# Block-sparse attention and mixture of experts on one core: the second half's dense tile moved to fourth place, and values stored batch by batch

## The chip, the cores and the metric

The kernel runs on one core of a Trainium2 chip. The metric is device time in microseconds (us), the median over runs. The core has a matrix engine (PE, its weight loads are listed as PEld), three engines for element-wise work (DVE, ACT, POOL), a queue engine SP that issues most transfers, and 16 DMA engines that carry them out.

## What is computed

The reference chains two parts. The first is attention over 4 batches, 8 heads, 768 tokens and head size 64, with a mask by blocks of 32 tokens (24 blocks): a block of queries sees its neighbours, the first and the last block, and three blocks that `sampled_blocks` names for it. The first and the last block of queries see everything.

```python
mask = np.abs(blk_i - blk_j) <= window
mask = mask | (blk_i == 0) | (blk_j == 0) | (blk_i == n_blocks - 1) | (blk_j == n_blocks - 1)
for qb in range(n_blocks):
    for kb in sampled_blocks[qb]:
        mask[qb * block:(qb + 1) * block, kb * block:(kb + 1) * block] = True
...
return np.matmul(attn, v).astype(np.float32)
```

The second part takes each of the 3072 output rows (512 wide), picks the best of 8 experts by gate logits plus a bias of the row's modality, and sends the row through that expert's two layers, scaled by the gate's weight.

```python
logits = x @ w_gate + modality_bias[modality_id]
e_idx = np.argmax(logits, axis=1)
...
    h = np.maximum(x[mask] @ w1[e], 0.0)
    out[mask] = gate_w[mask, None] * (h @ w2[e])
```

## The kernel before, in words

**Tiles.** The rows are cut into 24 tiles of 128 rows, 12 for each half, a half being two of the four batches. One tile of a half is dense: the first and the last block of both batches, with scores against all 768 keys. The other 11 are sparse: two neighbouring blocks of queries of both batches, m = 0 to 10. `tau_of` (L1236) numbers the tiles: the dense tile of a half is its tile 0, sparse tile m is tile m + 1.

**Items and stages.** The attention part is one list, `items` (L1249 to L1254), and the prediction uses an item's place t in it as a clock. The 8 dense items of the first half (2 batches with 4 pairs of heads each) stand at t = 0 to 7. Then come the 88 sparse items, four for each sparse tile, and the 8 dense items of the second half are put between them, two at a time, behind the sparse items that `DENSE_AFTER` lists. Before the change they stand at t = 30, 31, 40, 41 (batch 2) and 58, 59, 62, 63 (batch 3). Each item passes through stages at fixed distances, `LAG`: S scores, M the maximum, X the exponential, T transposes, A the copy out of PSUM, W and V the products with the values, O the division, Y and G the gate. In one step t every stage works on the item that is due, in the order `ORDER`. A dense item's product with the values (`dense_weigh`, L446, matmuls L451) comes 7 steps after its scores (L401); its transposes are L433. A sparse tile's scores are L557, its transposes L582, its products with the shared value blocks L604 (5 steps on) and with its own sampled blocks L613 (7 steps on).

**Loads.** SP issues them in program order; a load whose buffer is still in use holds back all that stand behind it. Keys and values of a batch for the dense tile are loaded whole: keys in 6 pieces (`dense_k`, L159), values in 6 pieces of 256 KB in rows of 2048 bytes (`dense_v`, L165). For the second half `DENSE_IN` says at which t the first of each six is issued, two steps apart. The keys of a batch also feed `share_k` (L480), where POOL copies key blocks for the sparse tiles, from t = 54 for the second half. A sparse tile's value blocks go into one of two buffers: `fetch_v` (L505, two blocks at L516 and L517, more for m = 0 and 1 at L511 to L514) and `fetch_own` (L539, six sampled blocks at L545), each block 128 KB. Values lie in memory as token, batch, feature, so that a block's row holds both batches of a half and is 4096 bytes. `fetch_v` for a tile stands 8 steps after the last item of the tile two before it, and waits for that tile's L613, which reads the same buffer.

**Routing.** When both tiles of a pair (2k, 2k + 1) have been gated, `routing` (L640) picks their experts, stores their rows to `x_d` and ranks them. After 16 tiles the fullest expert is chosen and its first 256 rows form an early group, and after 18 tiles a second one (`choose`, L1091), so that expert work starts before attention ends. `rows_of` (L1055) turns the rank table into row numbers to gather and row numbers to store, on DVE, three times (twice for 2 columns, once for 38). Behind the attention part PE multiplies expert groups of 256 rows without a break (L810 to L812, L825 to L827).

Of the kernel before, what the change touches and what calls it, by code (L numbers as in the profile page):

```python
# [15 lines left out]
ALU = mybir.AluOpType  # L16
# [4 lines left out]
P = 128  # L21
B, H, S, D = 4, 8, 768, 64
BLK = 32
NB = S // BLK
NPAIR = H // 2
HD = H * D
# [3 lines left out]
NT = NTOK // P  # L30
# [8 lines left out]
HB = 2  # L39
# [18 lines left out]
DENSE_DVE = ((0, 0), (0, 1))  # L58
DENSE_AFTER = (21, 29, 45, 47)
LAG = {'d': {'S': 0, 'M': 1, 'X': 2, 'T': 4, 'A': 4, 'W': 7, 'O': 8, 'V': 101, 'Y': 11, 'G': 13}, 's': {'S': 0, 'M': 1, 'X': 2, 'T': 4, 'A': 4, 'W': 5, 'V': 7, 'O': 8, 'Y': 10, 'G': 13}}  # L60
# [13 lines left out]

DENSE_IN = ((19, 14, 30), (49, 38, 44))
Q_IN = 22
# [14 lines left out]
def attention_moe(ctx, tc, kD, qD, qH, v0, v1, blocks, modality, w_gate, bias, w1, w2, out):  # L91
    nc = tc.nc
# [29 lines left out]
    with ExitStack() as actx:  # L122
# [13 lines left out]
        kd, vd = {}, {}  # L136
        KD_SLOT, VD_SLOT = (0, 1, 2, 9), (2, 3, 3, 3)
        ad = slot(4)
# [22 lines left out]
        def dense_v(b, ts=(0, 3), n=3):  # L161
            if b not in vd:
                vd[b] = slot(VD_SLOT[b])[:, 0:3072].rearrange("p (t f) -> p t f", t=6)
            for t in ts:
                nc.sync.dma_start(vd[b][:, t:t + n, :], vH[b // HB][t * P:(t + n) * P, b % HB].rearrange("(t p) f -> p t f", p=P))  # L165

# [336 lines left out]


        def fetch_v(m, half):  # L505
            i, g = 2 * m + 1, half * NM + m
            vg = vbuf[g % 2]
            vrow = vH[half].rearrange("(j s) b f -> s j (b f)", s=BLK)
            if m < 2:
                for n, j in ((0, 0), (1, NB - 1)):  # L510
                    nc.sync.dma_start(vg[32 + 32 * n:64 + 32 * n, 1, :], vrow[:, j, :])  # L511
            if m == 0:
                nc.sync.dma_start(vg[0:32, 1:3, :], vrow[:, i:i + 3:2, :])
                nc.sync.dma_start(vg[96:P, 0:2, :], vrow[:, i - 1:i + 2:2, :])  # L514
                return
            nc.sync.dma_start(vg[0:32, 2, :], vrow[:, i + 2, :])  # L516
            nc.sync.dma_start(vg[96:P, 1, :], vrow[:, i + 1, :])  # L517

# [20 lines left out]
        def fetch_own(m, half, n):  # L539
            i, g = 2 * m + 1, half * NM + m  # L540
            vg = vbuf[g % 2]
            vrow = vH[half].rearrange("(j s) b f -> s j (b f)", s=BLK)
            for k in ((0, 2, 1), (2, 0, 1))[n]:
                reg = own[g][3 * n + k]
                nc.sync.dma_start(vg[32 * (k + n):32 * (k + n) + 32, 2 * n, :], vrow[:, bass.ds(reg, 1), :].rearrange("p j f -> p (j f)"))  # L545

# [508 lines left out]
        def rows_of(tp, n, g_, s_, hold=None):  # L1055
            i_, f_ = ((lambda name, dt=dt: small.tile([P, NCOL], dt, name=name, bufs=1)[:, 0:n]) for dt in (I32, F32))
            pad, tf, to = f_("pad"), f_("tf"), f_("to")
            tk, tb, tn = i_("tk"), i_("tb"), i_("tn")
            nc.vector.tensor_scalar(to, tp[:, 0:n], 0.5, float(NTOK // 2 - 1), ALU.is_lt, ALU.add)
            yield  # L1060
            nc.vector.tensor_tensor(g_, tp[:, 0:n], to, ALU.add)
            if hold is not None:
                ready[NEAR] = True
                while not hold:
                    yield
            yield
            nc.vector.tensor_scalar(pad, tp[:, 0:n], 0.0, 8192.0, ALU.is_equal, ALU.mult)
            nc.vector.tensor_scalar(tk, g_, 7, None, ALU.logical_shift_right)
            yield
            nc.vector.tensor_scalar(tn, g_, 5, 1, ALU.logical_shift_right, ALU.bitwise_and)  # L1070
            nc.vector.tensor_scalar(tf, tk, float(NB // 2), float(-NB // 2), ALU.is_ge, ALU.mult)
            yield
            nc.vector.tensor_scalar(tb, g_, 6, 1, ALU.logical_shift_right, ALU.bitwise_and)
            nc.vector.tensor_tensor(tf, tf, tk, ALU.add)
            yield
            nc.vector.scalar_tensor_tensor(pad, tb, float(S - 2 * BLK), pad, ALU.mult, ALU.add)
            nc.vector.tensor_tensor(to, tf, tn, ALU.add)
            yield
            nc.vector.tensor_scalar(to, to, 0.5, float(S), ALU.is_le, ALU.mult)
            yield  # L1080
            nc.vector.scalar_tensor_tensor(to, tf, float(-2 * BLK), to, ALU.mult, ALU.add)
            yield
            nc.vector.scalar_tensor_tensor(to, g_, float(-BLK), to, ALU.add, ALU.add)
            yield
            nc.vector.tensor_tensor(s_, to, pad, ALU.add)
# [150 lines left out]
        def tau_of(m, half):  # L1236
            return half * (NT // 2) + m + 1

        def end_tile(m, half):
            tau = tau_of(m, half)  # L1240
            gate(tau, turns.pop((m, half)))
            gated.add(tau)
            if tau ^ 1 in gated:
                t = tau - tau % 2
                fillers.append(routing(t, lgs.pop(t), [xrs.pop((t % (NT // 2) + n - 1, half)) for n in range(2)]))

# [262 lines left out]
```

## Time and profile before

| | us |
|---|---|
| median of 3 runs | 526.32 |
| lowest and highest of them | 525.06, 530.39 |
| the profiled execution, whole | 523.66 |
| its span, first to last instruction | 521.9 |
| PE busy in the span | 499.5 |

The profile records one execution. Durations in the prediction are its own, and are set against its 523.66 us, of which 1.76 us lie outside the span. "issue" as the reason of an idle time means that the engine waited for nothing that the profile shows.

### The profile page before, as it was taken

To read this page: it belongs to the slowest core of one execution; us is meant where nothing else is said; L and a number is where in the kernel's file an instruction comes from. 1 tells how busy PE (TensorE), PEld (TensorE's weight loads), DVE (VectorE), ACT (ScalarE), POOL (GpSimd) and SP (SyncE) were. 2 spreads that over 40 slices of the span, in tenths; PEclk is the share of its full clock that TensorE was granted. 3 is DMA by queue.
4 is the path that set the end of the run, shared out by engine and by line. 5 is a ranking of instruction groups with operands and counts; after the bars stand their busy time and mean duration, and the time that the engine had idled before them with its cause. 6 is when DMAs were issued, how large, how long until landed. Compare 5 with 4: busy or idle time off the path is not lost.

```text
span 521.9 us, 18958 instructions
## 1 busy us (share of the span) xinstructions
PE 499.5 (96%) x7124; PEld 420.6 (81%) x7124; DVE 388.4 (74%) x1136; ACT 335.5 (64%) x765; POOL 244.9 (47%) x514
## 2 busy tenths in 40 slices
PE   7999999989899999899999999999999999999995
PEld 5667776767778777688989798998989899898974
DVE  5886688686689899967986868667686766768573
ACT  3799787978789978844545655555565545655561
POOL 6779685576458884312275051323324222241423
PEclk9999999999999999999999999999999999999999
DMA  8997885999756778965878797879669696877860
GB/s 293 332 249 227 241 222 184 244 228 258 196 174 191 207 219 245 273 192 200 242 281 294 246 297 258 266 233 301 200 240 284 227 295 202 280 223 251 260 209 25
DMA packets 59063, 123.84 MB, mean 237 GB/s; under 512 B 9681, under 2 KB 17618, under 8 KB 58962
## 3 DMA queue, kind: packets, MB, share of 16 engines
q1 hardware_dynamic: 54704, 108.88, 68.7%
q0 software_dynamic: 4256, 13.65, 7.9%
q8 instruction: 58, 0.95, 0.8%
q14 instruction: 43, 0.35, 0.3%
q10 hardware_dynamic: 2, 0.00, 0.0%
HBM read 105.97 MB, written 12.86 MB: 228 GB/s over the span
## 4 chain that ended last, share of the span: by engine, by line
PE 73%; DMA 11%; DVE 7%; ACT 3%; SPq 2%; issue 2%; POOL 0%; DVEq 0%; POOLq 0%; ACTq 0%
PE bank L810 8%; PE bank L812 8%; PE bank L811 8%; PE bank L827 7%; PE bank L826 7%; PE bank L825 7%; PE bank L557 6%; PE bank L582 6%; DMA slot<-x_d,gi 5%; PE bank L604 3%; PE bank L613 3%; PE bank L451 2%; DMA slot<-w 2%; PE bank L630 2%; PE bank L401 2%
## 5 line engine op out<-in xcount | busy, mean ns | idle before, releaser
L755 DVE TENSOR_TENSOR slot<-slot 128x1024 fp32r<-128x1024 f32 x99 | 124.6, 1272 | 63.1 <-ACT slot L752 54.9
L752 ACT CAST slot<-slot 128x1024 fp32r<-128x1024 f32 x104 | 107.0, 1047 | 68.3 <-PE bank L811 49.5
L810 PE MATMUL bank<-slot 128*128 128x256 f32 x384 | 108.4, 282 | 0.2 <-issue 0.2
L812 PE MATMUL bank<-slot 128*128 128x256 f32 x384 | 107.9, 281 | 0.1
L811 PE MATMUL bank<-slot 128*128 128x256 f32 x384 | 107.6, 280 | 0.0
L573 ACT ACTIVATE a<-y,mn 128x256 f32<-128x256 f32 x176 | 88.7, 511 | 7.9 <-DVE mn L565 7.7
L846 POOL DMA_INDIRECT out<-slot,si x20 | 27.3, 1364 | 109.5 <-ACT slot L842 106.5
L827 PE MATMUL bank<-slot 128*128 128x512 f32 x192 | 75.9, 395 | 0.4 <-DVE slot L818 0.4
L826 PE MATMUL bank<-slot 128*128 128x512 f32 x192 | 75.9, 395 | 0.0
L825 PE MATMUL bank<-slot 128*128 128x512 f32 x192 | 75.8, 395 | 0.0
L810 PEld LDWEIGHTS bank<-slot 128*128 128x128 f32 x384 | 72.3, 188 | 0.6
L811 PEld LDWEIGHTS bank<-slot 128*128 128x128 f32 x384 | 72.2, 188 | 0.6
L812 PEld LDWEIGHTS bank<-slot 128*128 128x128 f32 x384 | 72.2, 188 | 0.3 <-DVE slot L755 0.3
L565 DVE CUSTOM_DVE_ANT_1 y<-bank,smask 128x256 f32<-128x256 f32 x176 | 66.2, 416 | 0.5 <-PE bank L557 0.3
L502 POOL COPY slot<-slot 128x128 f32 x264 | 63.6, 293 | 0.0
L527 POOL TENSOR_SCALAR slot<-slot 32x1024 f32<-32x1024 f32 x40 | 41.7, 1042 | 33.2 <-issue 12.8
L587 ACT COPY at<-bank 128x512 f32<-128x512 f32 x88 | 50.6, 576 | 9.0 <-PE bank L582 9.0
L582 PE MATMUL bank<-ident,a 128*128 128x128 f32 x352 | 52.1, 280 | 3.0 <-issue 2.2
L557 PE MATMUL bank<-slot,q_raw 64*32 64x256 f32 x1408 | 48.7, 382 | 0.0
L582 PEld LDWEIGHTS bank<-ident,a 128*128 128x128 f32 x352 | 38.1, 141 | 7.3 <-issue 2.3
L827 PEld LDWEIGHTS bank<-slot 128*128 128x128 f32 x192 | 36.1, 188 | 9.2 <-DVE slot L818 0.9
L826 PEld LDWEIGHTS bank<-slot 128*128 128x128 f32 x192 | 36.0, 188 | 8.3 <-DVE slot L755 0.4
(307 smaller groups left out, 859.8 us busy)
## 6 DMA issues: line engine op xcount, KB each, us to landing
slot<-w SPq DMA_DIRECT2D x100, 512.0 KB, 5.2
slot<-v SPq DMA_DIRECT2D x180, 128.0 KB, 4.0
x_d<-xr SPq DMA_DIRECT2D x22, 256.5 KB, 4.2
q_raw<-qH SPq DMA_DIRECT2D x22, 256.0 KB, 4.8
slot<-v SPq DMA_DIRECT2D x16, 256.0 KB, 5.1
slot<-slot SPq DMA_DIRECT2D x120, 32.0 KB, 4.4
slot<-kD SPq DMA_DIRECT2D x13, 256.0 KB, 3.6
slot<-v SPq DMA_DIRECT2D x4, 768.0 KB, 12.4
```

What stands on the lines that cost most here:

```text
L557: nc.tensor.matmul(sp[u][32 * pr:32 * pr + 32, b * 256:(b + 1) * 256], lhsT=q[r, b * NPAIR + pr, n, :], rhs=kv[r, s0:s0 + 8, b, pr, :], st ...
L565: nc.vector.tensor_tensor_reduce(y[:, u, :].rearrange("p (s f) -> p s f", s=8), sp[u][:, b * 256:(b + 1) * 256].rearrange("p (s f) -> p s ...
L573: nc.scalar.activation(a[:, u, :], y[:, u, :], AF.Exp, bias=mn[:, u:u + 1], scale=-1.0, accum_out=total[:, u:u + 1])
L582: nc.tensor.transpose(tp[:, k:k + P], a[:, u, c * P:(c + 1) * P], ident)
L752: nc.scalar.copy(h, s)
L755: (eng or (nc.gpsimd if n in POOL_SPLITS else nc.vector)).tensor_tensor(l, s, h.bitcast(F32), ALU.subtract)
L810: nc.tensor.matmul(o, lhsT=h[:, fs], rhs=xh[g % 2][:, c, :], start=c == 0 and f % 2 == 0, stop=False)
L811: nc.tensor.matmul(o, lhsT=h[:, fs], rhs=xl[g % 2][:, c, :], start=False, stop=False)
L812: nc.tensor.matmul(o, lhsT=l[:, fs], rhs=xh[g % 2][:, c, :], start=False, stop=c == 3 and f % 2 == 1)
L825: nc.tensor.matmul(o, lhsT=hh[0][:, f, ts_], rhs=h[:, fs], start=f == 0, stop=False)
L826: nc.tensor.matmul(o, lhsT=hh[0][:, f, ts_], rhs=l[:, fs], start=False, stop=False)
L827: nc.tensor.matmul(o, lhsT=hl[f // 4][:, f % 4, ts_], rhs=h[:, fs], start=False, stop=f == 7)
```

## The change

Three things are edited together. The dense tile of the second half becomes tile 3 of its half (tau 15 instead of 12), and its items stand at t = 44, 45, 52, 53 (batch 2) and 64, 65, 68, 69 (batch 3); its loads have other times, and the values of batch 3 go to another buffer (slot 0, that of batch 0's keys, instead of slot 3, that of batch 2's values). Values lie in memory as batch, token, feature, so each block's row is two rows of 2048 bytes for all loads of `fetch_v` and `fetch_own`, and the two loads of two blocks each for m = 0 become four of one block. `rows_of` has to undo the other numbering of tiles, with seven more DVE instructions in each call.

```diff
-DENSE_AFTER = (21, 29, 45, 47)
+DENSE_AFTER = (35, 41, 51, 53)
+DENSE_PLACE = (0, 3)
-DENSE_IN = ((19, 14, 30), (49, 38, 44))
+DENSE_IN = ((38, 14, 20), (57, 26, 32))
-        KD_SLOT, VD_SLOT = (0, 1, 2, 9), (2, 3, 3, 3)
+        KD_SLOT, VD_SLOT = (0, 1, 2, 9), (2, 3, 3, 0)
...
-                nc.sync.dma_start(vd[b][:, t:t + n, :], vH[b // HB][t * P:(t + n) * P, b % HB].rearrange("(t p) f -> p t f", p=P))
+                nc.sync.dma_start(vd[b][:, t:t + n, :], vH[b // HB][b % HB, t * P:(t + n) * P].rearrange("(t p) f -> p t f", p=P))
...
+        def vblock(half, j):
+            rows = vH[half].rearrange("b (j s) f -> s b j f", s=BLK)
+            return rows[:, :, bass.ds(j, 1) if not isinstance(j, int) else slice(j, j + 1), :].rearrange("s b j f -> s b (j f)")
...
+            def rows_in(r, c, j):
+                nc.sync.dma_start(vg[r, c, :].rearrange("p (b f) -> p b f", b=HB), vblock(half, j))
...
-                nc.sync.dma_start(vg[32 * (k + n):32 * (k + n) + 32, 2 * n, :], vrow[:, bass.ds(reg, 1), :].rearrange("p j f -> p (j f)"))
+                nc.sync.dma_start(vg[32 * (k + n):32 * (k + n) + 32, 2 * n, :].rearrange("p (b f) -> p b f", b=HB), vblock(half, reg))
...
+            d, first = DENSE_PLACE[1], NT // 2
+            nc.vector.tensor_scalar(dj, tk, float(first), None, ALU.is_ge)
+            yield
+            nc.vector.tensor_scalar(to, tk, float(first + d), float(-d - 1), ALU.is_ge, ALU.mult)
+            nc.vector.tensor_tensor(dj, dj, to, ALU.add)
+            nc.vector.tensor_scalar(to, tk, float(first + d + 1), float(d), ALU.is_ge, ALU.mult)
+            nc.vector.tensor_tensor(dj, dj, to, ALU.add)
             nc.vector.scalar_tensor_tensor(pad, tb, float(S - 2 * BLK), pad, ALU.mult, ALU.add)
             nc.vector.tensor_tensor(to, tf, tn, ALU.add)
+            nc.vector.tensor_tensor(to, to, dj, ALU.add)
...
+            nc.vector.scalar_tensor_tensor(to, dj, float(2 * BLK), to, ALU.mult, ALU.add)
...
-            return half * (NT // 2) + m + 1
+            return half * (NT // 2) + (DENSE_PLACE[half] if m < 0 else m + (m >= DENSE_PLACE[half]))
```

How the order of instructions moves is shown at three places. The first is on PE, around the products with its own value blocks of the first half's last sparse tile (t = 62). Before, the row L613 is that product, L401 are dense scores, L433 dense transposes, L557 and L582 scores and transposes of sparse items:

```order
L433 MATMUL bank<-ident,a 128x128 x6
L401 MATMUL bank<-slot,qd 64x512 x4
L401 MATMUL bank<-slot,qd 64x256 x4
L597 MATMUL bank<-rexp,fold 32x8 x4
L613 MATMUL bank<-slot,at 32x64 x32
L433 MATMUL bank<-ident,a 128x128 x6
L582 MATMUL bank<-ident,a 128x128 x4
L557 MATMUL bank<-slot,q_raw 32x256 x16
```

After the change the same product is L622, sparse scores and transposes are L566 and L591, dense scores L402, the dense product with the values L452:

```order
L452 MATMUL bank<-slot 64x64 x12
L613 MATMUL bank<-slot,at 64x64 x16
L591 MATMUL bank<-ident,a 128x128 x8
L566 MATMUL bank<-slot,q_raw 32x256 x16
L639 MATMUL bank<-wg_raw,xT 64x8 x8
L606 MATMUL bank<-rexp,fold 32x8 x4
L622 MATMUL bank<-slot,at 32x64 x32
L591 MATMUL bank<-ident,a 128x128 x8
L402 MATMUL bank<-slot,qd 64x512 x4
```

The dense scores and transposes of batch 3 that stood around this product have left; the dense work that stands there now is the last product of batch 2, and batch 3's first scores follow behind.

The second place is the first product of batch 2 with its values on PE, with the waits (DMAHW names a transfer's landing). Before:

```order
L451 MATMUL bank<-slot 64x64 [waits DVE_49]
L451 MATMUL bank<-slot 64x64 x7
L451 MATMUL bank<-slot 64x64 [waits DMAHW4_49]
L451 MATMUL bank<-slot 64x64
L451 MATMUL bank<-slot 64x64 [waits DMAHW3_49]
```

After, where the row in front is the ranking of four tiles:

```order
L354 MATMUL bank<-oh,onesb 128x8
L452 MATMUL bank<-slot 64x64 [waits DVE_49]
L452 MATMUL bank<-slot 64x64 x5
L452 MATMUL bank<-slot 64x64 [waits DMAHW1_49]
L452 MATMUL bank<-slot 64x64
L452 MATMUL bank<-slot 64x64 [waits DMAHW5_49]
```

The product now waits for its last three value pieces one by one, instead of for two; the sixth piece is issued at t = 48 for a product at t = 51, where before it was t = 29 for t = 37.

The third place is on DVE, in `rows_of` of the first early group (gi_e holds the row numbers to gather, L755 is the subtraction that splits a weight, L565 and L574 a sparse item's maximum). Before:

```order
L1073 TENSOR_SCALAR tb<-gi_e_78 128x2
L1074 TENSOR_TENSOR tf<-tf,tk 128x2
L1076 SCALAR_TENSOR_TENSOR pad<-tb,pad 128x2
L1077 TENSOR_TENSOR to<-tf,tn 128x2
L755 TENSOR_TENSOR slot<-slot 128x1024
```

After, from behind the sparse item's maximum on:

```order
L1088 TENSOR_SCALAR to<-tk 128x2
L1089 TENSOR_TENSOR dj<-dj,to 128x2
L1090 TENSOR_SCALAR to<-tk 128x2
L1091 TENSOR_TENSOR dj<-dj,to 128x2
L1092 SCALAR_TENSOR_TENSOR pad<-tb,pad 128x2
L1093 TENSOR_TENSOR to<-tf,tn 128x2
L1094 TENSOR_TENSOR to<-to,dj 128x2
L1096 TENSOR_SCALAR to<-to 128x2
L459 TENSOR_SCALAR rt<-bank 128x8
```

The chain of row numbers is longer by the instructions on dj, and its later steps stand half a step t further back, just in front of a sparse tile's division (L459).

## Rows read from the trace of the kernel before

**Rows 1.** The page's first part: PE, busy us, share of the span, instructions.

```profile
PE 499.5 (96%) x7124; PEld 420.6 (81%) x7124; DVE 388.4 (74%) x1136; ACT 335.5 (64%) x765; POOL 244.9 (47%) x514
```

**Rows 2.** Windows: stretch, its length, busy us by engine, PE clock, DMA share, GB/s.

```profile
46.00:134.00 88.00, 80.80 (x2083) 61.23 (x2068) 65.57 (x295) 71.10 (x230) 59.36 (x159) 1.00 0.86 233
134.00:206.00 72.00, 71.67 (x1918) 55.65 (x1915) 62.02 (x305) 61.70 (x199) 49.76 (x136) 1.00 0.70 203
```

**Rows 3.** Waits of PE, whole span: line, what it waited for, us, times, longest.

```profile
PE bank L604 <- issue: 2.9, 5, 1.1
PE bank L582 <- issue: 2.2, 1, 2.2
...
PE bank L433 <- issue: 1.5, 1, 1.5
```

**Rows 4.** Windows of 8 us and less busy ones, same columns as rows 2.

```profile
110.00:118.00 8.00, 5.82 (x175) 4.24 (x175) 6.85 (x29) 5.65 (x19) 7.59 (x16) 1.00 0.99 234
118.00:126.00 8.00, 7.75 (x194) 5.70 (x191) 5.22 (x20) 6.13 (x20) 3.92 (x16) 1.00 1.05 279
126.00:134.00 8.00, 6.47 (x143) 5.10 (x144) 6.26 (x29) 6.17 (x21) 5.71 (x17) 1.00 1.00 236
134.00:142.00 8.00, 8.00 (x183) 6.39 (x181) 4.79 (x25) 7.02 (x23) 1.94 (x6) 1.00 0.63 176
198.00:206.00 8.00, 7.95 (x216) 5.99 (x212) 7.77 (x41) 6.84 (x21) 3.26 (x4) 1.00 0.87 272
222.00:230.00 8.00, 6.89 (x135) 6.18 (x135) 5.34 (x26) 3.67 (x6) 1.98 (x2) 1.00 0.46 139
```

**Rows 5.** Timeline of PE: start, us, instructions [idle before, and what ended it].

```profile
115.47 0.77 PE L582 MATMUL bank<-ident,a 128*128 128x128 f32 x5 [2.18 <-issue]
...
131.40 0.33 PE L433 MATMUL bank<-ident,a 128*128 128x128 f32 x1
133.20 0.70 PE L433 MATMUL bank<-ident,a 128*128 128x128 f32 x5 [1.48 <-issue]
```

**Rows 6.** The chain that ended last, in order of time: start, us, what.

```profile
61.98 1.45 PE bank L401 x16
63.61 0.92 PE bank L613 x64
...
71.57 1.12 PE bank L613 x64
...
128.92 1.45 PE bank L401 x16
```

**Rows 7.** Timeline of SP's queue at 84 to 92 us: start, us, issue.

```profile
85.78 0.33 SPq L516 DMA_DIRECT2D slot<-v  x1
...
88.99 2.33 SPq L545 DMA_DIRECT2D slot<-v  x3
91.37 0.41 SPq L159 DMA_DIRECT2D slot<-kD  x1
```

**Rows 8.** Issue to landing, median us: loads issued at 102 to 118, then 118 to 134.

```profile
slot<-v SPq DMA_DIRECT2D x4, 256.0 KB, 4.4
...
slot<-v SPq DMA_DIRECT2D x4, 256.0 KB, 6.3
```

**Rows 9.** L744 (rows of 4096 bytes), then L748 (2048): landing us, issue ns.

```profile
L744 SPq DMA_DIRECT2D slot<-w x48: 332/346/499, 232.9 to 490.7; - x48
DMA to landing us min/median/max: 3.6/5.3/6.8
...
L748 SPq DMA_DIRECT2D slot<-w x52: 367/383/471, 229.8 to 502.7; - x52
DMA to landing us min/median/max: 3.7/5.2/7.4
```

**Rows 10.** DVE in the timeline at 207 us, one instruction of rows_of's first call.

```profile
207.03 0.15 DVE L1083 SCALAR_TENSOR_TENSOR to<-gi_e,to 128x2 f32<-128x2 int32 x1
```

**Rows 11.** Waits of POOL at 100 to 125 us, same columns as rows 3.

```profile
POOL slot L488 <- DMA slot<-kD: 2.1, 1, 2.1
```

More of the change, by code (lines that the diff above doesn't have):

```diff
@@ L507, in fetch_v @@
             vg = vbuf[g % 2]
-            vrow = vH[half].rearrange("(j s) b f -> s j (b f)", s=BLK)
+            def rows_in(r, c, j):
+                nc.sync.dma_start(vg[r, c, :].rearrange("p (b f) -> p b f", b=HB), vblock(half, j))
             if m < 2:
                 for n, j in ((0, 0), (1, NB - 1)):
-                    nc.sync.dma_start(vg[32 + 32 * n:64 + 32 * n, 1, :], vrow[:, j, :])
+                    rows_in(slice(32 + 32 * n, 64 + 32 * n), 1, j)
             if m == 0:
-                nc.sync.dma_start(vg[0:32, 1:3, :], vrow[:, i:i + 3:2, :])
-                nc.sync.dma_start(vg[96:P, 0:2, :], vrow[:, i - 1:i + 2:2, :])
+                for n in range(2):
+                    rows_in(slice(0, 32), 1 + n, i + 2 * n)
+                for n in range(2):
+                    rows_in(slice(96, P), n, i - 1 + 2 * n)
                 return
-            nc.sync.dma_start(vg[0:32, 2, :], vrow[:, i + 2, :])
-            nc.sync.dma_start(vg[96:P, 1, :], vrow[:, i + 1, :])
+            rows_in(slice(0, 32), 2, i + 2)
+            rows_in(slice(96, P), 1, i + 1)
         shared = []
@@ L541, in fetch_own @@
             vg = vbuf[g % 2]
-            vrow = vH[half].rearrange("(j s) b f -> s j (b f)", s=BLK)
             for k in ((0, 2, 1), (2, 0, 1))[n]:
                 reg = own[g][3 * n + k]
-                nc.sync.dma_start(vg[32 * (k + n):32 * (k + n) + 32, 2 * n, :], vrow[:, bass.ds(reg, 1), :].rearrange("p j f -> p (j f)"))
+                nc.sync.dma_start(vg[32 * (k + n):32 * (k + n) + 32, 2 * n, :].rearrange("p (b f) -> p b f", b=HB), vblock(half, reg))
         def scores(q, g, n):
@@ L1056, in rows_of @@
             i_, f_ = ((lambda name, dt=dt: small.tile([P, NCOL], dt, name=name, bufs=1)[:, 0:n]) for dt in (I32, F32))
-            pad, tf, to = f_("pad"), f_("tf"), f_("to")
+            pad, tf, to, dj = f_("pad"), f_("tf"), f_("to"), f_("dj")
             tk, tb, tn = i_("tk"), i_("tb"), i_("tn")
@@ L1236, in tau_of, with tile_of @@
         def tau_of(m, half):
-            return half * (NT // 2) + m + 1
+            return half * (NT // 2) + (DENSE_PLACE[half] if m < 0 else m + (m >= DENSE_PLACE[half]))
+        def tile_of(tau):
+            half, n = divmod(tau, NT // 2)
+            return (-1 if n == DENSE_PLACE[half] else n - (n > DENSE_PLACE[half])), half
         def end_tile(m, half):
@@ L1244, in end_tile @@
                 t = tau - tau % 2
-                fillers.append(routing(t, lgs.pop(t), [xrs.pop((t % (NT // 2) + n - 1, half)) for n in range(2)]))
+                fillers.append(routing(t, lgs.pop(t), [xrs.pop(tile_of(t + n)) for n in range(2)]))
         dense = [[("d", b, pr) for b in (2 * h, 2 * h + 1) for pr in range(NPAIR)] for h in range(2)]
@@ L1486 @@
     k, q = cols(inputs["k"]), cols(inputs["q"])
+    order = [h * (NT // 2) + n for h, d in enumerate(DENSE_PLACE) for n in (*range(1, d + 1), 0, *range(d + 1, NT // 2))]
     arrays = {
@@ L1491 @@
             0, 3, 1, 2, 4, 5, 6, 7)).reshape(2, NM, P, 4 * P),
-        **{f"v{n}": np.ascontiguousarray(np.asarray(inputs["v"])[HB * n:HB * n + HB].transpose(2, 0, 1, 3)).reshape(S, HB, HD) for n in range(2)},
+        **{f"v{n}": np.ascontiguousarray(np.asarray(inputs["v"])[HB * n:HB * n + HB].transpose(0, 2, 1, 3)).reshape(HB, S, HD) for n in range(2)},
         "blocks": np.ascontiguousarray(inputs["sampled_blocks"]),
@@ L1495 @@
             np.asarray(inputs["moe_modality_id"]).reshape(2, HB, NB, BLK), 1, axis=2).reshape(2, HB, NB // 2, 2, BLK).transpose(
-                1, 3, 4, 0, 2)).reshape(P, NT),
+                1, 3, 4, 0, 2).reshape(P, NT)[:, order]),
         "w_gate": np.ascontiguousarray(inputs["moe_w_gate"]),
```

## The prediction

> **What bounds the kernel now.** I read the page's busy times first. PE works 499.5 us of a span of 521.9 [rows 1], so only 22.4 us can be won without removing matmuls, and the change removes none: the places of 8 dense items in a list change, the list's length doesn't. Next I cut the span into stretches, to see where PE idles near the edited items [rows 2]. From 46 to 134 us, where the second half's dense items and their loads stand, PE is busy 80.80 of 88 us: 7.20 us idle. From 134 to 206, sparse tiles alone, it is busy 71.67 of 72: 0.33 idle. The reader is to see the last two columns as well: DMA share 0.86 against 0.70. So the edited stretch loses 7.2 us and its neighbour, without dense items, nothing.
>
> What is waited for there? PE's waits name no engine for the largest ones: "issue", 2.9 us at L604, 2.2 at L582, 1.5 at L433 [rows 3]. The timeline puts the two longest at 115.47 and 133.20, after 2.18 and 1.48 us, the second one inside a run of six equal transposes, behind the first of them, where nothing of the program's data can be late [rows 5]. In stretches of 8 us, PE loses 2.18 at 110 to 118, 0.25 at 118 to 126 and 1.53 at 126 to 134, with DMA shares of 0.99, 1.05 and 1.00, and nothing at 134 to 142 with 0.63 [rows 4]. I take it that PE is held up now and then where the DMA engines are full. That is a coincidence of two columns, not a cause shown.
>
> To turn steps t into time I use the dense scores at t = 30 and t = 62, at 61.98 and 128.92 us [rows 6]: 66.94 us in 32 steps, 2.09 us a step.
>
> **The change part by part.** *Moved loads.* Before, batch 3's six key pieces go out at t = 38 to 48 and its six value pieces at t = 49 to 59. After, t = 45 to 53 (93 to 110 us) holds the last two value pieces of batch 2 only, where it held two key and three value pieces. So the DMA engines should come to 110 us without a queue, and the gap of 2.18 us should go. Bounds: 0 if the gap has another cause, -2.2 if it goes. I take -2.2. Batch 3's values now stand at t = 57 to 67 (118 to 139 us), beside the first tiles of the second half, which load most: 12 blocks of 128 KB for m = 0, 10 for m = 1, 8 for m = 2. The 1.53 us of 126 to 134 stay, and the saturated time grows by four steps, 8 us, out of a stretch that was idle on the DMA side (0.63). Bounds: 0 if it fits, +2.2 if it costs another gap as long as the longest. I take half, +1.1.
>
> *Keys earlier.* POOL waited 2.1 us for batch 3's keys in `share_k` [rows 11]. They now come 24 steps sooner, so this wait goes. No row has PE waiting for that copy, so it is worth 0, and what is late next on POOL is a buffer that PE still reads. The other buffer of batch 3's values removes a tie to batch 2's product; no wait of PE or POOL hung on it: 0.
>
> *Batch 2's values later.* This adds a wait. The sixth piece goes out at t = 48, the product that reads it is due at t = 51, where before there were 8 steps between. SP reaches the load so: it waits for the own-block product (L613) of t = 46, then issues two value blocks, a query load and three own blocks. In the trace the same sequence begins at 85.78 and the load behind it goes out at 91.37, 5.6 us later [rows 7]; landing takes 4.4 to 6.3 us [rows 8]. So the piece lands 10.0 to 11.9 us after that L613 ends. PE gets there like this: L613 ends at 64.53 and the next one at 72.69, a tile of four steps with two dense items in it, 8.16 us [rows 6]. Behind it come four transposes and the ranking, about 0.8 us by five transposes in 0.77 [rows 5], and the product reads the pieces in order, so the sixth is needed some 9.5 us after. PE therefore waits 0.5 to 2.4 us, and with it everything queued behind that product on PE, batch 2's next dense scores first. The lower bound is 0, if SP is quicker. I take 1.0, near the landing of 4.4 us, since SP's load is light at t = 45 to 53. Batch 3's sixth piece is issued right behind two value blocks at t = 67, for t = 71: about 1 + 6.3 us after L613 against the same 9.5: 0.
>
> *Seven more DVE instructions in each of three calls.* One takes 0.15 us [rows 10], so a call takes 1.1 us more. The first call ends at 207 us, and from 198 to 206 DVE is busy 7.77 of 8 us [rows 4]: of the 1.1 us only 0.23 fit beside other work. Queued behind them is a sparse tile's division, which frees a bank that PE needs. Bounds: 0 and +1.1; I take +0.9. The second call lies at 222 to 230, where DVE is busy 5.34 of 8: hidden, 0, at most +1.1. The third makes row numbers for stores that are issued much later: 0.
>
> *Rows of 2048 bytes.* The trace has one pair that differs in this alone: 512 KB of expert weights in rows of 4096 land in 5.3 us, in rows of 2048 in 5.2 [rows 9]. So the value blocks should land as before: 0. Issuing costs SP 383 against 346 ns, 0.04 us for each of eight blocks, 0.3 us a tile of 8.4 us; SP waits for PE at each tile, so that is hidden, and it is in the upper bound above.
>
> The Trainium skill speaks against this edit. Its page "Perfetto Trace Analysis", section "DMA Optimizations", calls small transfers costly and advises going from 2 KB to 4 KB or 8 KB where DMA bounds; the edit goes the other way. By the pair above the sum keeps its 0; by that rule it would get a positive term, which is a rival below.
>
> The sum: -2.2 + 1.1 + 1.0 + 0.9 = +0.8 us. Against the profiled execution that is 523.66 + 0.8 = 524.5; the median shown lies 2.66 above that execution, so for a median I say 526.32 + 0.8 = **527.1 us**. The bounds of the terms add up to -2.2 on one side and 2.2 + 2.4 + 1.1 + 1.1 = +6.8 on the other, but hardly all at once; the forecast's own range is 523.8 to 530.6.
>
> **The rivals.** *The full stretches dissolve (faster).* If the idle time of 46 to 134 us is all made by full DMA engines, and the new spacing of loads keeps them below that, PE idles there as from 134 to 206: 88 x 0.33 / 72 = 0.4 us instead of 7.2, with no wait for batch 2's values and DVE's extra work in the shade: 526.3 - 6.8 = 519.5. For it: share and idle time go together. Against it: batch 3's values stand at the busiest tiles, and the dense items themselves have long chains that move with them.
>
> *The queue at 118 to 147 us (slower).* From t = 57 to 71 the loads are 30 value blocks of 128 KB, six pieces of 256 KB, three query loads and four row stores of about 256 KB: 7.3 MB in 14 steps, 29.3 us. At 279 GB/s, the best of the full stretches, that takes 26 us; at 236 GB/s, the others' rate [rows 4], 31 us. Then the queue is 1.8 us behind and PE idles in each 8 us as at 126 to 134: 3.7 x 1.53 = 5.6 us where it was 1.8. With the later landings batch 2 and its successors cost 2.4: 1.8 + 3.8 + 2.4 + 0.9 - 2.2 = +6.7, 533.0. It decides from the point where DMA share stays at 1 to 147 us. For it: 236 is the rate of two of the three full stretches. Against: the stretch behind it has share 0.63 and can absorb a queue.
>
> *Short rows cost rate (slower, too).* Should value blocks take half as long again, then, with about 9 of the 14.6 MB that 134 to 206 moves being value blocks (8.6 tiles of eight), its share rises from 0.70 to 0.92, and PE idles there too, by the mean of the three full stretches 1.3 us in 8: +11.9, about 539 with the sum. Against it stands [rows 9]. The rule of "Perfetto Trace Analysis" named above points to this one.
>
> **How the numbers follow.** Forecast 0.70, dissolved 0.12, queue 0.14, short rows 0.04. One per cent is 5.3 us, about what a measurement of this kernel tells from no change: below 521.1 is faster, above 531.6 slower. Of the dissolved case two thirds lie below, with 0.01 of the forecast: 0.09. Of the queue case 0.08 lie above, with short rows 0.04 and 0.01 of the forecast: 0.13. The rest is 0.78. The range 521 to 532 leaves out 0.08 below and about 0.11 above.
>
> **What would show it.** In the profile after: PE idle from 46 to 134 us near 7; no wait of POOL for keys; no "issue" gap of 2 us near 113; a wait of PE for value pieces at the dense product near 106 us, 1 us long; DMA share near 1 to about 140 us; DVE fuller at 203 to 207. Landing of the 128 KB blocks unchanged. The prediction is wrong if value blocks land later everywhere, if the dense product waits much longer than 2.4 us, or if PE's "issue" gaps go altogether.

## The result: slower by 1.3%, and the profile after

The changed kernel took 532.40 us (median of 6 runs, 529.52 to 536.06) against 525.06 for the kernel before on the same chip (6 runs): ratio 1.0132, 95% interval 1.0094 to 1.0171. That is above the 1% within which the prediction had put it, and 0.4 us outside its range.

The profiled execution took 536.06 us, 12.4 us more than that of before. The difference of medians is 7.3, so what follows shows more of each loss than a median run has. Executions more than 1.5% above the fastest one of their kernel are left out of every ratio, clock and span x clock below; medians have all. First the page's busy times of the kernel after (answers [rows 1]):

```profile
PE 506.2 (95%) x7124; PEld 424.4 (79%) x7124; DVE 389.7 (73%) x1157; ACT 336.6 (63%) x765; POOL 250.1 (47%) x514
```

Windows of the kernel after, columns as in [rows 2]. The first ends at the first expert matmul, which comes at 238.42 us, 12.2 later than before:

```profile
0.00:238.40 238.40, 217.46 (x5232) 165.06 (x5232) 176.10 (x844) 183.12 (x575) 149.40 (x415) 0.98 0.78 222
...
46.00:134.00 88.00, 79.19 (x1986) 59.72 (x1986) 57.63 (x280) 68.07 (x220) 58.01 (x158) 0.96 0.76 210
134.00:206.00 72.00, 68.75 (x1770) 53.00 (x1766) 56.70 (x272) 58.17 (x187) 47.16 (x129) 1.00 0.71 195
...
62.00:98.00 36.00, 32.72 (x873) 24.32 (x861) 24.88 (x115) 28.46 (x92) 23.54 (x62) 1.00 0.87 234
98.00:134.00 36.00, 30.75 (x707) 23.16 (x697) 22.34 (x114) 24.93 (x82) 20.21 (x62) 0.91 0.67 187
...
104.00:111.20 7.20, 3.74 (x136) 2.89 (x134) 3.52 (x21) 4.70 (x16) 5.62 (x16) 1.00 0.84 225
111.20:118.00 6.80, 5.51 (x48) 3.09 (x50) 2.16 (x13) 1.68 (x5) 0.00 (x0) 0.50 0.92 246
118.00:126.00 8.00, 8.00 (x225) 6.56 (x222) 6.33 (x28) 6.21 (x19) 4.42 (x15) 1.00 0.34 104
126.00:134.00 8.00, 7.50 (x171) 5.60 (x162) 5.89 (x33) 7.47 (x26) 4.78 (x18) 1.00 0.43 134
...
142.00:158.00 16.00, 13.42 (x312) 9.84 (x310) 9.17 (x38) 11.42 (x37) 7.96 (x26) 1.00 0.97 225
...
234.10:237.50 3.40, 3.05 (x30) 2.51 (x33) 1.86 (x9) 2.01 (x5) 0.00 (x0) 0.50 0.97 253
```

The same for the kernel before, where the first expert matmul comes at 226.22:

```profile
0.00:226.20 226.20, 211.10 (x5232) 161.07 (x5232) 178.32 (x827) 181.39 (x574) 149.19 (x415) 1.00 0.82 234
...
62.00:98.00 36.00, 34.25 (x856) 25.80 (x858) 28.16 (x125) 29.61 (x97) 22.45 (x58) 1.00 0.77 221
98.00:134.00 36.00, 31.68 (x825) 24.11 (x822) 26.42 (x120) 28.08 (x92) 24.28 (x71) 1.00 0.96 240
...
142.00:150.00 8.00, 8.00 (x222) 6.19 (x221) 5.82 (x32) 5.92 (x19) 5.57 (x15) 1.00 0.44 143
150.00:158.00 8.00, 8.00 (x217) 6.39 (x216) 6.54 (x36) 6.59 (x23) 4.12 (x16) 1.00 0.64 194
```

Up to the first expert matmul PE has the same 5232 instructions in both, so the 12.2 us split cleanly: idle time 238.40 - 217.46 = 20.94 against 226.20 - 211.10 = 15.10, **5.8 us more idle**; busy time **6.4 us more** for the same instructions. The reason for most of the second is in the clock column. Between 111.2 and 118.0 and again between 234.1 and 237.5 us the granted clock is 0.50, that is 1.2 GHz instead of 2.4. PE works 5.51 + 3.05 = 8.56 us in these stretches; sixteen matmuls that take 1.45 us at full clock take 2.84 us there (below), so an estimated 4.2 us of the 8.56 are lost. The profile of before has no such stretch ahead of its last 4 us. The other 2.2 us of busy time are not explained; the profile of batch2_moved, one of the experiments, has 2.9 us more than before up to there, too, at a clock of 1.00.

The waits of PE in the kernel after (answers [rows 3]) name one place above all. Beside it, PE waits 2.7 and 1.2 us for the sparse tiles' value blocks at their products (L622, L613), for which it waits nowhere in the profile of before:

```profile
PE bank L452 <- DMA slot<-v: 4.8, 1, 4.8
PE bank L622 <- DMA slot<-v: 2.7, 4, 1.1
PE bank L622 <- issue: 2.0, 2, 1.5
...
PE bank L613 <- issue: 1.6, 2, 1.2
...
PE bank L613 <- DMA slot<-v: 1.2, 2, 0.8
```

The first row is batch 2's first product with its values. In PE's timeline after (the first row is a sparse tile's product with its own blocks, which frees a buffer for SP), the last 4 of 24 matmuls wait for the sixth piece; the idle time ends inside the first stretch at half clock, and the dense scores behind it (L402, x16) take 2.84 us, where before they took 1.45 [rows 6]:

```profile
97.23 1.40 PE L622 MATMUL bank<-slot,at 128*32 128x64 f32 x64
...
106.94 0.80 PE L452 MATMUL bank<-slot 128*64 128x64 f32 x20
112.49 0.48 PE L452 MATMUL bank<-slot 128*64 128x64 f32 x4 [4.75 <-DMA slot<-v]
...
113.95 2.84 PE L402 MATMUL bank<-slot,qd 64*64 64x512 f32 x16
```

The prediction's own route to that piece was SP's queue [rows 7]. SP's timeline after, with L166 the value pieces, L515 and L554 the sparse tiles' blocks, L147 a query load, L1319 a store:

```profile
97.04 1.33 SPq L554 DMA_DIRECT2D slot<-v  x3
98.41 0.44 SPq L166 DMA_DIRECT2D slot<-v  x1
99.03 1.31 SPq L554 DMA_DIRECT2D slot<-v  x3
100.39 1.42 SPq L166 DMA_DIRECT2D slot<-v  x1
101.91 0.37 SPq L1319 DMA_DIRECT2D x_d<-xr  x1
102.39 0.91 SPq L515 DMA_DIRECT2D slot<-v  x2
104.14 0.35 SPq L147 DMA_DIRECT2D q_raw<-qH  x1
106.02 2.32 SPq L554 DMA_DIRECT2D slot<-v  x3
108.39 0.42 SPq L166 DMA_DIRECT2D slot<-v  x1
```

The stretch from the two blocks to the piece takes 6.0 us (5.6 in the prediction), and the piece lands 4.1 us after its issue (4.4). Both durations held. What did not is the start: the two blocks go out at 102.39, 3.8 us after the product that frees their buffer ended (97.23 + 1.40), since SP still has five loads and stores of the steps before to issue (99.03 to 101.91). So the piece is issued at 108.39, 0.65 us after PE had stopped for it. SP is behind, and what it waited for on the way is not PE: its longest wait, 1.7 us at 94.7 us, is put down to POOL (L489, the key copies in `share_k`), the shorter ones mostly to landings of earlier transfers (SP's waits after, 84 to 110 us):

```profile
SPq L515 <- POOL slot L489: 1.9, 2, 1.7
SPq L147 <- DMA slot<-v: 0.8, 1, 0.8
SPq L554 <- DMA slot<-v: 0.6, 1, 0.6
...
SPq L166 <- DMA slot<-v: 0.3, 1, 0.3
```

### The profile page after: what moved, and what is told of

Its sections match the earlier page's. It is cut to its first block, busy times and chain, and to the rows that moved or that the text cites. A ratio compares the mean times of both kernels' runs of the same rounds, so it can differ in the third digit from the quotient of the medians.

```text
span 534.3 us, 18983 instructions
## 1 busy us (share of the span) xinstructions
PE 506.2 (95%) x7124; PEld 424.4 (79%) x7124; DVE 389.7 (73%) x1157; ACT 336.6 (63%) x765; POOL 250.1 (47%) x514
## 2 busy tenths in 40 slices
DMA packets 65143, 123.84 MB, mean 232 GB/s; under 512 B 9745, under 2 KB 17682, under 8 KB 65042
## 4 chain that ended last, share of the span: by engine, by line
PE 63%; DMA 14%; DVE 10%; SPq 6%; issue 3%; ACT 2%; POOL 1%; POOLq 0%; DVEq 0%; ACTq 0%
PE bank L836 8%; PE bank L835 8%; PE bank L834 8%; PE bank L819 7%; PE bank L821 7%; PE bank L820 7%; DMA slot<-v 5%; DMA slot<-x_d,gi 4%; PE bank L566 4%; PE bank L591 4%; DVE y L574 2%; SPq L554 2%; PE bank L452 2%; PE bank L622 2%; PE bank L402 2%
## 5 line engine op out<-in xcount | busy, mean ns | idle before, releaser
L764 DVE TENSOR_TENSOR slot<-slot 128x1024 fp32r<-128x1024 f32 x99 | 121.2, 1237 | 59.1 <-ACT slot L761 49.2
L582 ACT ACTIVATE a<-y,mn 128x256 f32<-128x256 f32 x176 | 88.3, 507 | 9.6 <-DVE mn L574 9.0
L574 DVE CUSTOM_DVE_ANT_1 y<-bank,smask 128x256 f32<-128x256 f32 x176 | 66.4, 417 | 0.5 <-PE bank L566 0.3
L591 PE MATMUL bank<-ident,a 128*128 128x128 f32 x352 | 53.1, 282 | 0.2
L566 PE MATMUL bank<-slot,q_raw 64*32 64x256 f32 x1408 | 49.5, 382 | 0.2 <-POOL slot L503 0.2
L591 PEld LDWEIGHTS bank<-ident,a 128*128 128x128 f32 x352 | 38.4, 142 | 5.7 <-ACT a L582 1.6
```

Source lines behind the costliest of these rows:

```text
L566: nc.tensor.matmul(sp[u][32 * pr:32 * pr + 32, b * 256:(b + 1) * 256], lhsT=q[r, b * NPAIR + pr, n, :], rhs=kv[r, s0:s0 + 8, b, pr, :], st ...
L574: nc.vector.tensor_tensor_reduce(y[:, u, :].rearrange("p (s f) -> p s f", s=8), sp[u][:, b * 256:(b + 1) * 256].rearrange("p (s f) -> p s ...
L582: nc.scalar.activation(a[:, u, :], y[:, u, :], AF.Exp, bias=mn[:, u:u + 1], scale=-1.0, accum_out=total[:, u:u + 1])
L591: nc.tensor.transpose(tp[:, k:k + P], a[:, u, c * P:(c + 1) * P], ident)
L764: (eng or (nc.gpsimd if n in POOL_SPLITS else nc.vector)).tensor_tensor(l, s, h.bitcast(F32), ALU.subtract)
```

## The experiments

Twelve kernels were run in three sets, each beside runs of the kernel before on its chip (525.12 us, 18 runs; 526.71, 35; 527.67, 29). A ratio holds across sets, a time only within its set. The last column is the median of span times mean granted clock: roughly the span that the run would have at full clock. It takes one random part out, and a little too much, since half clock costs nothing while PE idles. It is 520.5, 520.6 and 521.1 us for the three sets of before, and 524.4 for the changed kernel.

| run | median us | ratio to before, 95% interval | granted clock | span x clock |
|---|---|---|---|---|
| changed kernel | 532.40 | 1.0132 (1.0094 to 1.0171) | 0.987 | 524.4 |
| rows_only | 527.09 | 1.0031 (0.9992 to 1.0070) | 0.992 | 519.6 |
| long_rows | 531.92 | 1.0122 (1.0083 to 1.0161) | 0.990 | 524.1 |
| v_early | 530.90 | 1.0097 (1.0052 to 1.0142) | 0.994 | 524.6 |
| long_rows_v_early | 531.54 | 1.0142 (1.0093 to 1.0191) | 0.992 | 525.8 |
| old_load_times | 530.16 | 1.0067 (1.0033 to 1.0101) | 0.993 | 524.3 |
| old_key_times | 531.59 | 1.0070 (1.0033 to 1.0107) | 0.994 | 524.6 |
| late_piece_alone | 525.84 | 0.9994 (0.9960 to 1.0028) | 0.993 | 522.0 |
| no_row_steps | 532.17 | 1.0089 (1.0054 to 1.0123) | 0.990 | 523.0 |
| before_no_loads | 521.04 | 0.9871 (0.9821 to 0.9922) | 0.994 | 516.6 |
| moved_no_loads | 524.15 | 0.9938 (0.9902 to 0.9973) | 0.994 | 518.4 |
| batch2_moved | 530.68 | 1.0034 (0.9991 to 1.0076) | 0.992 | 521.5 |
| batch3_moved | 531.60 | 1.0091 (1.0053 to 1.0130) | 0.991 | 524.2 |

### The two first suspects: the late piece and the short rows

*rows_only* is the kernel before with the values stored batch by batch (one of the loads; the others are changed in the same way):

```diff
...
-                nc.sync.dma_start(vg[32 * (k + n):32 * (k + n) + 32, 2 * n, :], vrow[:, bass.ds(reg, 1), :].rearrange("p j f -> p (j f)"))
+                nc.sync.dma_start(vg[32 * (k + n):32 * (k + n) + 32, 2 * n, :].rearrange("p (b f) -> p b f", b=HB), vblock(half, reg))
...
```

> The kernel before with the values stored batch by batch and nothing else (dense tile, its loads and the row numbers as before). Theory A (the late sixth value piece of batch 2, issued 3 steps ahead of its product, costs PE 4.75 us of idle time and about 3.4 us more at half clock): the piece is early here, so 525 us, PE without waits for value blocks and the granted clock at 1.00 throughout attention. Theory B (rows of 2048 bytes make the value blocks land later everywhere): 529 to 532 us, waits of PE for value blocks of 3 us or more at the products with shared and own blocks, POOL waiting more than 8 us for value blocks.

*long_rows* is the changed kernel with that edit taken back, *v_early* the changed kernel with the six pieces issued five steps sooner, *long_rows_v_early* both. The edit of the first (its main line), then of the second:

```diff
...
-            rows = vH[half].rearrange("b (j s) f -> s b j f", s=BLK)
+            rows = vH[half].rearrange("(j s) b f -> s j (b f)", s=BLK)
...
```

```diff
-DENSE_IN = ((38, 14, 20), (57, 26, 32))
+DENSE_IN = ((33, 14, 20), (57, 26, 32))
```

> The changed kernel with the values stored by token again, so that a block's row is one of 4096 bytes (the dense tile is still the fourth, with its load times). Theory A: the late piece is still late, PE still waits 2 us or more at batch 2's product with its values, and the time stays at 529 to 532 us. Theory B: SP is no longer behind when it reaches the sixth piece, that wait falls to 1 us or less, the other waits of PE for value blocks go, and the time is 525 to 527 us.

> The changed kernel with batch 2's value pieces issued from step 33 instead of 38, so that the sixth is 8 steps ahead of its product as before the change. Theory A: the 4.75 us wait and the half clock behind it go, about 8 us in the profile, 524 to 526 us. Theory B: that one wait goes (4 to 5 us with or without a part of the half clock), but the waits at products with shared and own blocks stay at 3 to 4 us and POOL's at 20 us or more: 528 to 530 us.

> The changed kernel with both: rows of 4096 bytes and batch 2's value pieces from step 33. Theory A: no different from early pieces alone, 524 to 526 us. Theory B: no different from rows of 4096 bytes alone, 525 to 527 us. If both causes count, it is lower than either alone by 1 us or more, at or below 525 us.

Theory B falls: short rows alone cost 0.3% with an interval that holds zero, and taking them back leaves 1.2%. Theory A falls as well: without the late piece 1.0% stay, without both 1.4%. The 4.75 us were real, and the wait is gone from the profile of long_rows_v_early. But that profile finds other idle time in its place: of 62 to 98 us PE is busy 31.45, in the kernel after 32.72. Nor do short rows by themselves make the value blocks late: in the profile of rows_only PE waits 0.5 us and POOL 9.0 us for them, against 0 and 8.1 in before. With the items moved, the waits are there with rows of 4096 bytes too, 2.4 and 15.9 us in long_rows.

### The late piece by itself

*late_piece_alone* puts the same lead of three steps into the kernel before:

```diff
-DENSE_IN = ((19, 14, 30), (49, 38, 44))
+DENSE_IN = ((24, 14, 30), (49, 38, 44))
```

> The kernel before with batch 2's value pieces issued from step 24 instead of 19, so that the sixth goes out 3 steps ahead of its product, as in the change. Theory A: PE waits at that product, near 76 us, 2 to 5 us for the piece; if an idle time of 4 us or more is what lowers the granted clock, the profile shows a stretch at 0.50 directly behind it. Time 3 to 8 us above before, 528 to 533. The rival: the wait is taken out of slack that PE has here anyway, the product 0.5 us late, and the time is 525 to 526 us.

The rival held, at 0.9994. Timeline of PE, then of SP, in that run:

```profile
76.18 0.80 PE L451 MATMUL bank<-slot 128*64 128x64 f32 x20 [0.52 <-DVE mn L565]
77.27 0.34 PE L451 MATMUL bank<-slot 128*64 128x64 f32 x4 [0.28 <-DMA slot<-v]
```

```profile
72.31 0.42 SPq L165 DMA_DIRECT2D slot<-v  x1
```

Here the piece goes out 4.7 us before PE reaches its matmul (0.80 after 76.18) and the wait is 0.28 us; in the changed kernel it goes out 0.65 us after. Three steps are not a lead in time: when SP really issues decides, and measured against PE's need that was 5.3 us worse at the new place. (The profile of this run has no long wait in it, so whether one would have lowered the clock here was not tested.) Nor is it the same in each execution: in the profile of no_row_steps, which has the changed kernel's loads, the 24 matmuls run through without a wait, in an execution of 526.13 us:

```profile
108.89 0.92 PE L452 MATMUL bank<-slot 128*64 128x64 f32 x24
```

### The loads' times, and the row numbers

*old_load_times* is the changed kernel with rows of 4096 bytes and every dense load at its step of before (values of batch 3 still in slot 0); *old_key_times* has only the keys there; *no_row_steps* is the changed kernel without the seven steps on dj. The edits in this order, without those for the rows:

```diff
-DENSE_IN = ((38, 14, 20), (57, 26, 32))
+DENSE_IN = ((19, 14, 30), (49, 38, 44))
```

```diff
-DENSE_IN = ((38, 14, 20), (57, 26, 32))
+DENSE_IN = ((33, 14, 30), (57, 38, 44))
```

```diff
-            nc.vector.tensor_scalar(dj, tk, float(first), None, ALU.is_ge)
...
-            nc.vector.tensor_tensor(to, to, dj, ALU.add)
...
-            nc.vector.scalar_tensor_tensor(to, dj, float(2 * BLK), to, ALU.mult, ALU.add)
```

> Dense items at their new places, rows of 4096 bytes, all dense loads of batches 2 and 3 at the steps they had before the change (values of batch 3 in slot 0). Neither short rows nor a late piece is left. Theory C (where the dense items stand costs the time, whatever their loads do): 529 to 532 us, as in the three runs with one or both of the other edits undone. Theory D (the crowding of dense loads into steps 14 to 43 costs it, by value blocks that land late for the tiles at 65 to 95 us): 524 to 526 us, and PE's waits for value blocks at the product with own blocks (0 before, 1.4 to 2.7 us in the runs at the new place) are gone.

> As the run with rows of 4096 bytes and early pieces, but all keys at the steps they had before (14 and 30 for batch 2, 38 and 44 for batch 3) and the values at 33 and 57. Theory C: 529 to 532 us. Theory D, if it is the early keys: 524 to 526 us; if it is the values: 529 to 532 us while the run with all old load times is at 524 to 526.

> The changed kernel without the seven DVE instructions that undo the other numbering of tiles in the row numbers (so rows are gathered and stored by the wrong numbers; all sizes are the same). Prediction's term: 0.9 us less than the changed kernel, 531 to 532 us, and the 1.1 to 1.7 us for which PE waits at the gate near 210 to 218 us are gone. Rival: hidden, no difference (532 us).

Theory D falls: 0.7% stay in both, with old load times too. Whether the load times are worth the step from the 1.2% of long_rows to these 0.7% is open, the intervals overlap. PE's timeline in old_load_times shows the kind of gap that the prediction took away at 113 us, now at 98 us and longer, with no data behind it:

```profile
97.14 1.08 PE L622 MATMUL bank<-slot,at 128*32 128x64 f32 x64
102.15 1.01 PE L591 MATMUL bank<-ident,a 128*128 128x128 f32 x4 [3.93 <-issue]
```

The window behind it, and the transfers of 98.2 to 102.2 us by queue:

```profile
101.40:108.20 6.80, 6.05 (x78) 4.50 (x79) 0.76 (x6) 3.54 (x12) 0.40 (x1) 0.50 0.74 206
```

```profile
q1 hardware_dynamic: 466, 0.99, 98.4%
q8 instruction: 1, 0.02, 2.0%
```

The clock is at 0.50 behind this gap too. In the gap the DMA engines are full of data, and among it is one transfer of the instruction queue.

The gap in front of these four transposes (L591 behind a product L622) is no single event. Every profile with batch 2's items moved and the dense loads left in has it, 1.39 to 3.93 us long (old_key_times 1.77, long_rows_v_early 1.90, v_early 3.38, batch2_moved 1.39), except the two in which PE stops some 9 us later for the sixth piece (the kernel after, 4.75 us, and long_rows, 3.50). no_row_steps, with the changed kernel's own loads, has it as well:

```profile
99.03 0.69 PE L591 MATMUL bank<-ident,a 128*128 128x128 f32 x4 [2.28 <-issue]
```

no_row_steps lies 0.4% (2.3 us) below the changed kernel, but the intervals overlap; the predicted 0.9 us is neither refuted nor measured. The wait that it was to cause does occur in some profiles: near 211 to 218 us PE's gate matmuls (L639) wait for a sparse tile's division on DVE (L459) for 1.69 us in long_rows, 1.59 in long_rows_v_early, 1.07 in v_early and 0.92 in old_load_times. It is in none of the six profiles without the seven steps, and missing from the other four with them, that of the kernel after among these.

### No dense loads at all

*before_no_loads* and *moved_no_loads* (rows of 4096 bytes) leave out the 24 dense loads of the second half:

```diff
...
-                side(DENSE_IN[b - 2][0] + 2 * t, lambda b=b, t=t: dense_v(b, (t,), 1))
...
+            side(DENSE_IN[b - 2][0], lambda b=b: vd.update({b: vd[b - 2]}))
+            side(DENSE_IN[b - 2][1], lambda b=b: kd.update({b: kd[b - 2]}))
```

> The kernel before without the dense loads of batches 2 and 3 (24 loads of 256 KB, 6.3 MB): their dense items read the keys and values of batches 0 and 1 instead, so the second half's result is of other data; every instruction on PE, ACT and DVE stays. If the gaps of 2.18 and 1.48 us at 113 and 132 us come from full DMA engines, they go: 3 to 5 us less than before, 520 to 522 us. If not, no difference.

> The changed kernel with rows of 4096 bytes and, in the same way, without the dense loads of batches 2 and 3. Theory E (the place costs because DMA engines are full at 62 to 98 us, beside sparse tiles that now follow each other without dense items between them): the place's cost goes with the loads, the time is that of the kernel before without loads plus 1 us for the row numbers, 521 to 523 us. Theory C (the place costs whatever the loads): 3 to 5 us above the kernel before without loads, 524 to 527 us.

Without the loads the kernel before is 1.3% faster. Its window of 46 to 134 us, then that of moved_no_loads:

```profile
46.00:134.00 88.00, 86.31 (x2195) 65.54 (x2202) 68.53 (x309) 75.56 (x245) 59.48 (x159) 1.00 0.66 187
```

```profile
46.00:134.00 88.00, 85.45 (x2217) 65.69 (x2214) 69.04 (x313) 76.13 (x247) 63.64 (x171) 1.00 0.70 187
```

7.20 us of idle time [rows 2] become 1.69, and the two waits at 113 and 132 us (L582 and L433 in [rows 3]) are gone, while the DMA share falls from 0.86 to 0.66. So they do hang on the dense loads that fill the DMA engines. But leaving loads out of one stretch does not end such gaps elsewhere: the same profile has one of 3.66 us at 215.8 to 219.4 us, some 80 us behind the place of these loads, where the engines are full (share 1.04), and half clock follows it. It is the longest of this row of PE's waits in before_no_loads:

```profile
PE bank L604 <- issue: 4.3, 3, 3.7
```

At the new place the loads' cost goes as well (2.55 idle), but the place's does not: 0.9938 / 0.9871 = 1.0068, 3.5 us, about the same 0.7% as with the loads at their old times. Set against each other directly, the 12 runs of moved_no_loads lie 3.1 us above the 6 of before_no_loads in the mean, 95% interval 0.9 to 5.3. Theory E falls, theory C stands, with the row-number steps still inside its cost.

### One batch at a time

*batch2_moved* moves batch 2's items alone (values from step 33, batch 3's in slot 0, numbers as before; rows of 4096 bytes); *batch3_moved* moves batch 3's alone and makes the dense tile the fourth, with the steps on dj (the edits cut to the places):

```diff
-DENSE_AFTER = (21, 29, 45, 47)
+DENSE_AFTER = (35, 41, 45, 47)
...
```

```diff
-DENSE_AFTER = (21, 29, 45, 47)
+DENSE_AFTER = (21, 29, 51, 53)
+DENSE_PLACE = (0, 3)
...
```

> The kernel before with batch 2's dense items alone at their new places (steps 44, 45, 52, 53; batch 3's stay at 58, 59, 62, 63), its values issued from step 33, batch 3's values in slot 0; rows of 4096 bytes, tile numbers and row numbers as before. Theory E: this is the part of the change that leaves 62 to 92 us without dense items, so it has most of the place's cost, 2 to 4 us above before. Rival: the cost is batch 3's, no difference here (within 1 us).

> The kernel before with batch 3's dense items alone at their new places (steps 64, 65, 68, 69) and the dense tile as the fourth of its half, with the seven steps for row numbers; all dense loads and rows as before. Theory E: only the row numbers' 1 us, 0 to 1.5 us above before. Rival: 3 to 4 us above.

Theory E finds no support here either: batch 2's move costs 0.3%, not told from zero, batch 3's with the new number of the tile and the row-number steps 0.9%. Together they make about the 1.2% of long_rows. But the runs do not tell the two moves apart: their intervals overlap, the medians of all 12 runs differ by 0.9 us, and the means by 0.8 us with a 95% interval of -1.7 to 3.4. What is shown is a cost of batch 3's move with all that goes with it. Whether it is the row-number steps, the place of batch 3's items or the tile's number was not separated: batch 3's move without the steps, and the steps alone in the kernel before, were not run. Also not tried: spreading the loads of the kernel before out of 98 to 134 us, which by before_no_loads could win up to 1.3%. No run beat the kernel before by more than its interval except those that leave the loads out.

## Why the prediction was wrong

The measured 532.40 lies only 0.4 us above the range of 521 to 532, but 5.3 us above the forecast of 527.1, and one of the prediction's own signs of being wrong came true: the dense product waited much longer than 2.4 us. Term by term:

**-2.2, the gap at 113 us.** The reading was right and the conclusion wrong. The gaps of [rows 5] hang on the dense loads, which the prediction called a coincidence of two columns: without these loads they are gone. In the changed kernel's profile no "issue" wait stands near 113 either. But the loads are all still there, and idle time came up elsewhere: of 62 to 98 us PE idled 1.75 us before and 3.28 after, of 134 to 206 us 0.33 [rows 2] and 3.25 (most of it beside batch 3's values, below). The gap itself moved with batch 2's items to 97 to 103 us, 2.28 us long in no_row_steps and 3.93 in old_load_times. Taking it out of the sum without asking where the queue goes was the first failed step.

**+1.0, the wait for the sixth piece.** The mechanism was right, at the place and line named, and the size wrong: 4.75 us against an upper bound of 2.4. The two durations it was built on held (6.0 us in SP's queue, 4.1 us to land). The failed premise is "SP's load is light at t = 45 to 53", by which SP would start that sequence when PE's product ends. SP had a backlog of five issues and started 3.8 us late. By itself the term was still no reason for the result: the same lead costs nothing in the kernel before, and taking it back gains at most 0.3%, which the intervals do not tell from nothing.

**Not in the sum: the clock.** [rows 2] and [rows 4] show 1.00 everywhere, and the prediction took it for fixed. That profile was a favourable one: its mean clock is 0.998, where the three sets of before have medians of 0.996, 0.994 and 0.992. In the profiled execution of the changed kernel an estimated 4.2 of 12.2 us are half clock. In the medians it is 0.987 at a span of 530.65 us, at most 6.9 us lost, against 2.1, 3.1 and 4.2 in the three sets of before (spans of 522.5, 524.5 and 525.1): 2.7 to 4.8 of the 7.3 us. The clock falls behind gaps, so this is a second price of the idle time rather than a cause of its own.

**Not in the sum: the place.** What is left by span x clock, 3.3 to 3.9 us (524.4 against 520.5 to 521.1), is found in every kernel with both batches moved: 2.5 to 5.3 us with loads, each against before in its set, and 1.9 us without (518.4 against 516.6). The prediction gave the move of PE's items no price of its own, only its loads. That was the second failed step. What in the new place costs the time stays open; of this rest, 0.9 us are the predicted row-number steps if that term is right.

**Short rows, 0.** Held: 1.0031, with zero inside the interval. The rule of the Trainium skill that spoke against it ("Perfetto Trace Analysis", section "DMA Optimizations") is not borne out at this size here: batch-by-batch values, 65143 packets instead of 59063, could not be told from the 4096-byte rows by time.

**+1.1, batch 3's values at 118 to 139 us.** The cost came, later than forecast. At 118 to 134 us the DMA share is 0.34 and 0.43 and PE idles 0.50 us, against 1.05 and 1.00 and 1.78 us before [rows 4]. But SP issued these pieces only at 131.5 to 150.5 us, and the full stretch came with them: at 142 to 158 us the share is 0.97 and PE idles 2.58 us, where before it was 0.44 and 0.64 with no idle time. 2.44 of the 2.58 us are two "issue" gaps (PE's timeline after):

```profile
150.05 0.40 PE L639 MATMUL bank<-wg_raw,xT 128*64 128x8 f32 x6 [0.93 <-issue]
...
156.91 0.65 PE L622 MATMUL bank<-slot,at 128*32 128x64 f32 x30 [1.51 <-issue]
```

From 118 to 158 us PE idles 3.08 us against 1.78 before, 1.3 us more, so in this execution the size fits the term.

**The rivals.** "The queue at 118 to 147 us" gave 533.0, the nearest number to the 532.4 measured, but its point of decision, a share of 1 to 147 us, did not occur as stated: the share was 0.34 to 0.43 at 118 to 134 us, and the full stretch came later and cost 2.58 us, where the rival had 5.6. A time that fits is no evidence for its mechanism. "Dissolved" did not happen in the change; before_no_loads shows that its mechanism exists at 46 to 134 us, and by its gap at 216 us that a load left out here does not end the gaps there.

## What to carry to other kernels

A load that is moved out of a full stretch is still a load: price the stretch that it moves into, and do not book the old gap as won. A lead counted in steps is worth what the issuing queue's backlog leaves of it, so read when that queue really issues, not when its release comes. And on PE a wait of several microseconds is paid twice if the granted clock falls behind it: here 4.75 us of waiting and, as an estimate, half of the 5.51 us of work in the stretch behind.

## What was not expected of the hardware

*The clock.* It fell to 0.50 behind the 4.75 us of idle time here, behind the 3.93 us in old_load_times and behind the 3.66 us in before_no_loads. In the kernel before it stayed at 1.00 behind 2.18 us, in no_row_steps it fell behind 2.28 us (0.50 at 99.4 to 102.8). Before, behind its gap:

```profile
115.50:119.00 3.50, 3.50 (x88) 2.79 (x88) 2.94 (x15) 2.84 (x9) 3.33 (x8) 1.00 1.02 283
```

But it also fell at 234.1 us in the kernel after, behind a shorter gap (PE's timeline):

```profile
233.33 0.57 PE L613 MATMUL bank<-slot,at 128*64 128x64 f32 x13 [1.19 <-issue]
```

So one gap's length does not decide it alone. The Trainium skill ("TensorE: Matmul & The Clock Gate", "Part 1: The HAM clock gate (the 'warmup' mystery)") says that half clock is the array's default, which only activity lifts; the three long gaps, of 3.66 to 4.75 us with 0.50 behind each, agree.

*"issue" as a wait for instructions.* Two of the gaps without a data releaser lie at transfers of the instruction queues (q8, q14) while data fill the engines: the data's share (q1) is 0.98 at the gap in old_load_times above, and 1.01 in the kernel before at 112.6 to 115.6 us, around its gap of 113.3 to 115.5:

```profile
q1 hardware_dynamic: 311, 0.72, 100.9%
q8 instruction: 1, 0.02, 2.1%
q14 instruction: 1, 0.01, 1.4%
```

The 3.66 us gap of before_no_loads holds one of q8 too. One such meeting tells little, since q8 has 16 transfers from 46 to 134 us in the kernel before, one in 5.5 us. That PE stood there because its next instructions came late is argued from this coincidence and from before_no_loads, not shown by a run that changes the instructions alone. The Trainium skill ("Runtime: NRT & Kernel Launch", section "Instruction fetch mechanics") describes such transfers in blocks of 16 KiB, mostly hidden; here, with full engines, idle times of 2.18 and 3.93 us stand at them.
